# Block-sparse attention and a gated MLP in one program: w_in's raw words in their parts' place, fetched five tiles ahead; w_out's store on SyncE; a pair's last values and turns behind the next pair's scores

## The chip, the cores and the metric

The kernel runs on one core of one Trainium2 chip. The metric is the device time of one execution in microseconds (us). One execution was also recorded by the hardware profiler, with every instruction of the five engines (TensorE = PE, VectorE = DVE, ScalarE = ACT, GpSimd = POOL, SyncE = SP) and every DMA.

## The reference, cut to what matters

```python
# q, k, v: (4, 8, 768, 64); block = 32, 24 blocks of queries and keys; 3 sampled blocks a row of blocks
scores = scale * q @ k.T
mask   = |blk_i - blk_j| <= 1, or blk_i / blk_j is the first or last block, or blk_j is sampled for blk_i
attn   = softmax(where(mask, scores, -1e9))
x      = (attn @ v) as (3072 tokens, 512)
h      = x @ w_in                                   # (512, 2048)
g      = h * (1.0 / (1.0 + np.exp(-1.702 * h)))
return g @ w_out                                    # (2048, 512)
```

The weights come as 64-bit floats; the kernel gets their raw words and makes 32-bit parts of them.

## The kernel before, in words

**Tokens and chunks.** The 3072 tokens are 48 units of 64 tokens (two blocks of queries each); 8 units make a chunk of 512 tokens, and there are 6 chunks. 44 units are sparse: one item of work each, which reads 8 gathered key blocks (tile `kg`) and the matching value rows (`vown`, gathered by index, and `vmid`, the fixed ones). The other units, first and last block, are dense and have several items.

**An item** has four PE parts. `scores` (L262, 32 matmuls into two PSUM banks) is followed by `least` on DVE (L285, four instructions: bias and row minimum) and `exps` on ACT (L297, four). `transposes` (L313, eight) turns the exponentials over, and ACT copies them out of two PSUM banks (L318, two copies into `wst` or `pt` tiles). `values` (L339, 64 matmuls) is followed by `normalise` on DVE (L381). `turn` (L392, two transposes) is followed by ACT's copy `xhi` (L399) and DVE's remainder `xlo` (L400), which the MLP reads.

**Order.** The order of the instructions on each engine is written out by hand: it is the order in which the Python code issues them. Each engine works its own queue strictly in that order, and DMAs wait on the queue of the engine that issues them.

**The stage of pairs**, `first()`: chunk 0's eight items go in four pairs. A pair's two `scores` come first, then DVE and ACT work on both, then both items' `transposes`, both items' `values`, both `turn`s. Each pair shares one entry of keys and one of values. Both rings have two places (`RING = 2`): `loads()` issues the loads of a new entry once the code has issued the last reader of the one whose place it takes (the DMA then waits for that reader). Loads of `vown` stand on POOL's queue, those of `vmid`, `qt` and most of `kg` on SP's. `hold()` keeps some loads back until a pair's row minima exist.

**The ticks**, `tick(m)`: after the pairs, tick m does one slice of 128 of the 2048 hidden columns for one chunk: `up` (L495 to L497, 12 matmuls), `gate` (ACT L503, L508; DVE L510), and `down` of the slice before. There are 16 ticks a chunk. While chunk c is in the MLP, chunk c+1's items are put between the ticks' matmuls by `plan()`, always at the same ticks: scores in one tick, transposes in the next, values of an item behind the scores of the following one. In chunk 0, `down` is a 32-bit matmul (L540); from chunk 1 on it uses split parts (L552, L556, L557).

**The weights**, the generator `weights()` (`self.conv`): while chunk 0 is in the MLP, 32 tiles of raw words, alternately w_in and w_out (`todo`), are made into 32-bit parts. For tile k: `fetch(k)` issues a DMA of 512 KB on POOL's queue into one of three `raw` buffers (L422); `first(k)` is an ACT instruction that reads the words (L434); DVE shifts (L444), merges the high word (L451) and the low word (L458). For w_in ACT copies the high part into `win[f]` (L461) and DVE writes the remainder (L448). For w_out the whole word is kept, and a DMA on POOL's queue stores it to `ws[f]` (L464), from where later chunks read it. `next(self.conv)` issues one step of this; `weights(n)` in `first()` and `run(n)` in `tick()` say how many. Before tile k's steps the code calls `fetch(k + 2)`; the buffer that it takes is the one that tile k - 1 has just been read from. `first(k + 1)` is issued in the middle of tile k's steps, so ACT's queue stands still there if tile k + 1's words have not landed.

Of the kernel before, what the change touches and what calls it, by code (L numbers as in the profile page):

```python
# [18 lines left out]
P = 128  # L19
# [19 lines left out]
BIG = float(2 ** 33)  # L39
SCALE = 1.0 / float(D) ** 0.5  # L40
REBASE = 2.0 ** -112


class Kernel:
# [4 lines left out]
    def __init__(self, ctx, tc, q, qd, kb, kT, v, vd, sb, w_in, w_out, out):  # L49
# [15 lines left out]
        self.qt = [c.tile([P, 2, NPAIR * UT], F32, name=f"qt{i}") for i in range(RING)]  # L65
        self.vown = [c.tile([P, 2, 2 * DM], F32, name=f"vown{i}") for i in range(RING)]
        self.vmid = [c.tile([P, 2 * DM], F32, name=f"vmid{i}") for i in range(RING)]
        self.win = [c.tile([P, 2 * DM], F32R, name=f"win{f}") for f in range(NF)]
        self.wout = [c.tile([P, 2 * DM], F32R, name=f"wout{i}") for i in range(WRING)]
        self.x = [(c.tile([P, NCT, CT], F32R, name=f"xhi{i}"), c.tile([P, NCT, CT], F32R, name=f"xlo{i}"))  # L70
                  for i in range(2)]
# [334 lines left out]
    def weights(self):  # L406

        nc = self.nc
        todo = []
        for f in range(NF + LAG):  # L410
            if f < NF:
                todo.append((f, 0))
            if f >= LAG:
                todo.append((f - LAG, 1))
        self.ready = set()
        tiles = {}

        def fetch(k):
            if k < len(todo):
                f, i = todo[k]  # L420
                raw = self.work.tile([P, 2 * DM], I32, name="raw", bufs=3)
                nc.gpsimd.dma_start(out=raw, in_=self.w64[i][f])  # L422
                tiles[k] = {"raw": raw.rearrange("p (a b) -> p a b", b=2)}

        def first(k):


            f, i = todo[k]
            if i == 0:
                a = self.work.tile([P, DM], I32, name="a")  # L430
            else:
                a = self.work.tile([P, DM], F32R, name=("ghi", "glo")[f % 2]).bitcast(I32)
            tiles[k]["a"] = a
            nc.scalar.activation(out=a.bitcast(F32), in_=tiles[k]["raw"][:, :, 1].bitcast(F32), func=AF.Abs, scale=REBASE)  # L434

        fetch(0)
        fetch(1)
        yield
        first(0)
        for k, (f, i) in enumerate(todo):  # L440
            fetch(k + 2)
            raw, a = tiles[k]["raw"], tiles[k]["a"]
            low, high = raw[:, :, 0], raw[:, :, 1]
            nc.vector.tensor_scalar(out=a, in0=a, scalar1=3, scalar2=None, op0=ALU.logical_shift_left)  # L444
            yield
            if k > 0 and todo[k - 1][1] == 0:
                t, w = self.win[todo[k - 1][0]], tiles[k - 1]["a"].bitcast(F32)
                nc.vector.tensor_tensor(out=t[:, DM:2 * DM], in0=w, in1=t[:, 0:DM].bitcast(F32), op=ALU.subtract)  # L448
                self.ready.add(todo[k - 1])
                yield  # L450
            nc.vector.scalar_tensor_tensor(out=a, in0=high, scalar=-0x80000000, in1=a, op0=ALU.bitwise_and,  # L451
                                           op1=ALU.bitwise_or)
            if k + 1 < len(todo):
                while todo[k + 1][1] == 1 and (not self.turned or todo[k + 1][0] - 4 > self.downs - 1):
                    yield
                first(k + 1)
            yield
            nc.vector.scalar_tensor_tensor(out=a, in0=low, scalar=29, in1=a, op0=ALU.logical_shift_right,  # L458
                                           op1=ALU.bitwise_or)
            if i == 0:  # L460
                nc.scalar.copy(out=self.win[f][:, 0:DM], in_=a.bitcast(F32))  # L461
            else:
                self.whole[f] = a.bitcast(F32)
                nc.gpsimd.dma_start(out=self.ws[f], in_=self.whole[f])  # L464
                self.ready.add((f, i))
            yield

# [210 lines left out]
    def first(self):  # L678
# [5 lines left out]
        def finish(todo):  # L684
            for f in todo:
                f()
# [5 lines left out]
        def hold(g, k):  # L692

            nc.gpsimd.tensor_copy(out=self.seen[:, 0:NPAIR], in_=g["unit"]["nm"][:, 0])
            self.vmost = k

        for p in range(CU // 2):
            pair = items[2 * p:2 * p + 2]
            exps = [self.scores(g) for g in pair]
            exps[0][0]()  # L700
            finish(exps[0][1:])
            exps[1][0]()
            exps[1][1]()
            if p == 0:
                hold(pair[1], CU // 2)
            if p == CU // 2 - 1:
                hold(pair[0], CU // 2 + 1)
                nc.sync.dma_start(out=self.seen[:, NPAIR:2 * NPAIR], in_=pair[0]["unit"]["nm"][:, 0])
                self.kmost = CU // 2 + 1
            self.loads()  # L710
            behind = [self.transposes(pair[0])]
            behind[0][0]()
            exps[1][2]()
            finish(behind[0][1:])
            behind.append(self.transposes(pair[1]))
            if p == CU // 2 - 1:
                self.turned = True
                weights(2)
            finish(behind[1])
            after = [self.values(g) for g in pair]  # L720
            finish(after[0])
            finish(after[1])
            self.loads()
            for g in pair:
                finish(self.turn(g))
            if p > 0:
                weights((1, 3, 2)[p - 1])

    def run(self):
        self.g, self.wst, self.whole, self.downs = {}, {}, {}, 0  # L730
# [63 lines left out]
```

## Time and profile before

| | |
|---|---|
| time, median of 3 runs | 803.52 us (802.85 to 808.4) |
| time of the profiled execution | 802.63 us |
| its span, first to last instruction | 801.0 us |
| PE, DVE, ACT, POOL busy | 755.8, 396.7, 365.4, 77.3 us |
| mean granted clock of TensorE | 0.980 |
| DMA | 128.20 MB, 160 GB/s over the span |

Busy shares are averages over stages that have different limits, so the rows further down are taken by stage: the pairs end where the first `up` starts, at 65.86 us; chunk 0's ticks end where the first split `down` (L556) starts, at 229.26 us; the rest is chunks 1 to 5. A wait is shown by who waited, for whom, and how long; a chain of waits is followed back from an end to what released each step.

### The profile page before, as it was taken

The numbers are of one execution on the slowest core, as the hardware profiler recorded it, in microseconds if no ns is written. First come the engines' busy times: TensorE is split into PE (matmuls) and PEld (weight loads), VectorE is DVE, ScalarE is ACT, GpSimd is POOL, SyncE is SP. The second block draws the span as 40 slices with busy tenths as digits, with TensorE's granted clock in tenths as the row PEclk, the third lists the DMA queues.
The fourth block names the chain that finished last, engine by engine and source line by source line (L and its number), as shares of the span: only waits on it lengthen the run. The fifth ranks groups of instructions, "written<-read, shape, count | busy, mean of one in ns | idle before, by whom it ended". The sixth has DMA issues, their size and how long they took to land.

```text
span 801.0 us, 19132 instructions
## 1 busy us (share of the span) xinstructions
PE 755.8 (94%) x7520; PEld 563.5 (70%) x7520; DVE 396.7 (50%) x1044; ACT 365.4 (46%) x919; POOL 77.3 (10%) x125
## 2 busy tenths in 40 slices
PE   3778799799999999999999999999999999999997
PEld 2545555565677777777878778778777777788885
DVE  4366667666355453454454454444555444443333
ACT  2464555444454545354444454454455444332332
POOL 3422222230000000000000000000000000000000
PEclk9889899899999999999999999999999999999999
DMA  8959877685574254655444365354574222132111
GB/s 259 296 184 348 256 256 226 238 283 162 156 246 158 76 161 150 204 155 171 137 122 159 117 170 175 112 179 119 159 244 157 89 70 75 41 92 54 40 53 52
DMA packets 61211, 128.20 MB, mean 160 GB/s; under 512 B 7713, under 2 KB 27938, under 8 KB 60610
## 3 DMA queue, kind: packets, MB, share of 16 engines
q1 hardware_dynamic: 47650, 80.90, 33.6%
q0 software_dynamic: 12656, 45.23, 17.0%
q8 instruction: 59, 0.97, 0.5%
q10 hardware_dynamic: 816, 0.86, 0.4%
q14 instruction: 30, 0.25, 0.1%
HBM read 116.47 MB, written 10.49 MB: 158 GB/s over the span
## 4 chain that ended last, share of the span: by engine, by line
PE 81%; DMA 8%; DVE 4%; ACT 3%; issue 3%; SPq 1%; POOL 0%; ACTq 0%; POOLq 0%; DVEq 0%
PE bank L495 11%; PE bank L497 10%; PE bank L496 10%; PE bank L556 9%; PE bank L557 9%; PE bank L552 9%; PE bank L339 5%; PE bank L313 5%; PE bank L262 5%; DMA raw<-in_moe_w_out_dram 3%; PE bank L540 3%; PE bank L347 2%; PE bank L274 2%; DMA raw<-in_moe_w_in_dram 1%; DMA kg<-in_kb_dram 1%
## 5 line engine op out<-in xcount | busy, mean ns | idle before, releaser
L495 PE MATMUL bank<-xhi,win 128*128 128x512 f32 x384 | 162.0, 422 | 1.9 <-ACT wst L508 1.3
L497 PE MATMUL bank<-xhi,win 128*128 128x512 f32 x384 | 151.1, 393 | 0.1
L496 PE MATMUL bank<-xlo,win 128*128 128x512 f32 x384 | 151.0, 393 | 0.0
L510 DVE SCALAR_TENSOR_TENSOR g<-g,bank 128x512 f32<-128x512 f32 x83 | 57.1, 687 | 187.6 <-ACT g L503 187.6
L297 ACT ACTIVATE ex<-bank,nm 128x256 f32<-128x256 f32 (+1 forms) x176 | 84.6, 489 | 123.7 <-DVE nm L285 122.0
L556 PE MATMUL bank<-wout,ghi 128*128 128x512 f32 x320 | 128.4, 401 | 0.0
L503 ACT ACTIVATE g<-bank 128x512 f32<-128x512 f32 x96 | 57.4, 598 | 153.7 <-PE bank L497 153.7
L557 PE MATMUL bank<-wout,ghi 128*128 128x512 f32 x320 | 126.7, 396 | 0.0
L484 DVE TENSOR_TENSOR wout<-wst,wout 128x512 fp32r<-128x512 f32 x80 | 55.4, 692 | 78.2 <-ACT wout L483 77.3
L552 PE MATMUL bank<-wout,glo 128*128 128x512 f32 x320 | 89.8, 394 | 0.0
L495 PEld LDWEIGHTS bank<-xhi,win 128*128 128x128 f32 x384 | 72.4, 188 | 23.9 <-ACT wst L508 3.2
L497 PEld LDWEIGHTS bank<-xhi,win 128*128 128x128 f32 x384 | 72.3, 188 | 16.1
L285 DVE CUSTOM_DVE_ANT_1 bank<-bank,bias 128x256 f32<-128x256 f32 x176 | 73.7, 441 | 19.9 <-PE bank L262 16.9
L496 PEld LDWEIGHTS bank<-xlo,win 128*128 128x128 f32 x384 | 72.5, 189 | 15.0 <-issue 2.2
L218 POOL DMA_INDIRECT vown<-in_v_dram,vidx x44 | 43.4, 986 | 390.1 <-PE bank L339 272.4
L262 PE MATMUL bank<-kg,qt 64*32 64x256 f32 x1408 | 55.2, 404 | 23.8 <-DMA kg<-in_kb_dram 12.5
L517 ACT CAST ghi<-g 128x512 fp32r<-128x512 f32 x80 | 49.6, 621 | 45.4 <-DVE g L510 45.4
L552 PEld LDWEIGHTS bank<-wout,glo 128*128 128x128 f32 x320 | 60.1, 188 | 14.5
L318 ACT COPY pt<-bank 128x512 f32<-128x512 f32 (+1 forms) x112 | 57.2, 562 | 28.1 <-PE bank L313 28.1
L557 PEld LDWEIGHTS bank<-wout,ghi 128*128 128x128 f32 x320 | 60.2, 188 | 13.7
L556 PEld LDWEIGHTS bank<-wout,ghi 128*128 128x128 f32 x320 | 60.1, 188 | 13.5
L262 PEld LDWEIGHTS bank<-kg,qt 64*32 64x32 f32 x1408 | 26.4, 111 | 47.6 <-issue 20.2
(103 smaller groups left out, 942.6 us busy)
## 6 DMA issues: line engine op xcount, KB each, us to landing
wst<-ws SPq DMA_DIRECT2D x80, 256.0 KB, 2.7
kg<-in_kb_dram SPq DMA_DIRECT2D x142, 128.0 KB, 3.5
kg<-in_kb_dram SPq DMA_DIRECT2D x22, 384.0 KB, 4.9
raw<-in_moe_w_in_dram POOLq DMA_DIRECT2D x16, 512.0 KB, 5.7
raw<-in_moe_w_out_dram POOLq DMA_DIRECT2D x16, 512.0 KB, 5.9
kg<-in_kT_dram SPq DMA_DIRECT2D x4, 1536.0 KB, 8.3
vown<-in_vd_dram SPq DMA_DIRECT2D x8, 768.0 KB, 4.5
qt<-in_q_dram SPq DMA_DIRECT2D x22, 256.0 KB, 3.4
```

Of the source, the lines that this page charges most:

```text
L262: nc.tensor.matmul(sps[h][BLK * c:BLK * (c + 1), n * i:n * (i + 1)].rearrange("p (n s) -> p n s", s=BLK), self.qt[r][rows, bi, UT * pair + ...
L285: nc.vector.tensor_tensor_reduce(out=at, in0=at, in1=bias, scale=-SCALE, scalar=3.0e38, op0=ALU.add, op1=ALU.min, accum_out=un["nm"][:, ha ...
L297: nc.scalar.activation(out=ex, in_=sps[h][:, n * k:n * (k + 1)], func=AF.Exp, bias=un["nm"][:, half, c:c + 1], scale=-1.0, accum_out=un["r ...
L318: copies.append(lambda pt=pt, ps=ps, m=m: nc.scalar.copy(out=pt[:, 0:m], in_=ps[:, 0:m]))
L495: nc.tensor.matmul(h, wih[:, k], hi[:, k], start=(k == 0), stop=False)
L496: nc.tensor.matmul(h, wih[:, k], lo[:, k], start=False, stop=False)
L497: nc.tensor.matmul(h, wil[:, k], hi[:, k], start=False, stop=(k == NCT - 1))
L503: nc.scalar.activation(out=g, in_=self.h, func=AF.Tanh, scale=0.851)
L510: nc.vector.scalar_tensor_tensor(out=g, in0=g, scalar=1.0, in1=h, op0=ALU.add, op1=ALU.mult)
L552: nc.tensor.matmul(o[n], glo[:, tk[n]], woh, start=False, stop=last)
L556: nc.tensor.matmul(o[n], ghi[:, tk[n]], woh, start=(f == 0), stop=False)
L557: nc.tensor.matmul(o[n], ghi[:, tk[n]], wol, start=False, stop=False)
```

## The change

`AHEAD = 5`: five fetches are issued at once, and tile k's steps begin with `fetch(k + 5)`. The raw words of w_in no longer go through the `raw` buffers: they land in the place of `win[f]` itself (the same const tile, as integers), and the tile of parts is allocated over it after the low words have been read. The three `raw` buffers are left to w_out's words. A further `yield` stands behind `first(0)`. The store of w_out's tile to `ws[f]` is issued by SyncE instead of GpSimd.

In `first()`, a pair ends with its first item's `values`. The second item's `values` and both `turn`s come behind the next pair's `scores`. Both items' `exps` are now all issued ahead of the first copy out of the transposes. `loads()` is called once for each pair instead of twice. Steps of `weights` are issued at other places: the fetches at the end of the third pair (before: of the second), the rest in and behind the last pair; no step of `weights` is left between the third pair and the fourth pair's scores.

```diff
+AHEAD = 5
...
-        self.win = [c.tile([P, 2 * DM], F32R, name=f"win{f}") for f in range(NF)]
+        self.win = [None] * NF
...
         def fetch(k):
             if k < len(todo):
                 f, i = todo[k]
-                raw = self.work.tile([P, 2 * DM], I32, name="raw", bufs=3)
+                if i == 0:
+                    raw = self.const.tile([P, 2 * DM], I32, name=f"win{f}")
+                else:
+                    raw = self.work.tile([P, 2 * DM], I32, name="raw", bufs=3)
                 nc.gpsimd.dma_start(out=raw, in_=self.w64[i][f])
...
-        fetch(0)
-        fetch(1)
+        for k in range(AHEAD):
+            fetch(k)
         yield
         first(0)
+        yield
         for k, (f, i) in enumerate(todo):
-            fetch(k + 2)
+            fetch(k + AHEAD)
...
             if i == 0:
+                self.win[f] = self.const.tile([P, 2 * DM], F32R, name=f"win{f}")
                 nc.scalar.copy(out=self.win[f][:, 0:DM], in_=a.bitcast(F32))
             else:
                 self.whole[f] = a.bitcast(F32)
-                nc.gpsimd.dma_start(out=self.ws[f], in_=self.whole[f])
+                nc.sync.dma_start(out=self.ws[f], in_=self.whole[f])
...
+        prev = None
         for p in range(CU // 2):
-            pair = items[2 * p:2 * p + 2]
-            exps = [self.scores(g) for g in pair]
+            a, b = items[2 * p:2 * p + 2]
+            final = p == CU // 2 - 1
+            exps = [self.scores(g) for g in (a, b)]
+            after, turned = (self.values(prev[1]), self.turn(prev[0])) if p else ([], [])
             exps[0][0]()
             finish(exps[0][1:])
             exps[1][0]()
-            exps[1][1]()
+            finish(exps[1][1:])
+            finish(after)
...
             self.loads()
-            behind = [self.transposes(pair[0])]
-            behind[0][0]()
-            exps[1][2]()
-            finish(behind[0][1:])
-            behind.append(self.transposes(pair[1]))
-            if p == CU // 2 - 1:
+            behind = self.transposes(a)
+            finish(turned)
+            if p:
+                finish(self.turn(prev[1]))
+            if final:
+                weights(1)
+            finish(behind)
+            behind = self.transposes(b)
+            if final:
                 self.turned = True
                 weights(2)
-            finish(behind[1])
-            after = [self.values(g) for g in pair]
-            finish(after[0])
-            finish(after[1])
-            self.loads()
-            for g in pair:
-                finish(self.turn(g))
-            if p > 0:
-                weights((1, 3, 2)[p - 1])
+            finish(behind)
+            if final:
+                weights(1)
+            finish(self.values(a))
+            if p == CU // 2 - 2:
+                weights(1)
+            prev = a, b
+        after = self.values(b)
+        turned = self.turn(a)
+        finish(after)
+        finish(turned)
+        finish(self.turn(b))
+        weights(3)
```

## Rows read from the trace of the kernel before

**Rows 1.** Busy time by stage (the windows view): stretch in us, its length, busy us and (x) instructions of PE, PE's weight loads, DVE, ACT, POOL, then granted TensorE clock, DMA share, GB/s.

```profile
12.48:65.86 53.38, 40.16 (x848) 27.87 (x848) 25.86 (x101) 28.09 (x92) 13.84 (x20) 0.84 0.84 264
65.86:229.26 163.40, 149.79 (x1445) 93.77 (x1446) 104.92 (x258) 79.60 (x200) 36.69 (x56) 0.96 0.73 237
229.26:801.00 571.74, 565.89 (x5229) 441.81 (x5227) 261.55 (x659) 256.20 (x628) 20.60 (x22) 1.00 0.42 127
```

**Rows 2.** The page's fourth part, the chain that ended last over the whole span, by line.

```profile
PE bank L495 11%; PE bank L497 10%; PE bank L496 10%; PE bank L556 9%; PE bank L557 9%; PE bank L552 9%; PE bank L339 5%; PE bank L313 5%; PE bank L262 5%; DMA raw<-in_moe_w_out_dram 3%; PE bank L540 3%; PE bank L347 2%; PE bank L274 2%; DMA raw<-in_moe_w_in_dram 1%; DMA kg<-in_kb_dram 1%
```

**Rows 3.** Waits of ACT between 64 and 205 us: who waited for whom, us in total, times, longest.

```profile
ACT a L434 <- DMA raw<-in_moe_w_in_dram: 15.1, 8, 4.7
...
ACT ghi L434 <- DMA raw<-in_moe_w_out_dram: 10.4, 4, 4.7
...
ACT glo L434 <- DMA raw<-in_moe_w_out_dram: 5.9, 2, 4.2
```

**Rows 4.** Four links of the chain of waits, in order of time: start us, us, what.

```profile
81.09 5.69 DMA raw<-in_moe_w_in_dram
86.86 0.66 ACT a L434
87.52 0.48 ACT pt L318
88.04 2.44 PE bank L262 x32
```

**Rows 5.** The largest wait of PE between 64 and 205 us.

```profile
PE bank L262 <- ACT pt L318: 10.1, 4, 4.3
```

**Rows 6.** The windows view of two stretches right behind such waits (columns as in rows 1; the last three are clock, DMA share, GB/s).

```profile
88.04:93.40 5.36, 5.36 (x98) 3.19 (x99) 4.82 (x14) 4.20 (x12) 0.67 (x2) 0.50 0.80 254
152.65:158.30 5.65, 5.65 (x99) 3.75 (x100) 5.51 (x18) 2.92 (x10) 1.07 (x2) 0.50 0.62 200
```

**Rows 7.** Two items' scores on PE's timeline: start us, us, line, out<-in, count, idle time before and its releaser.

```profile
105.15 1.09 PE L262 MATMUL bank<-kg,qt 64*32 64x256 f32 x32
...
134.64 1.78 PE L262 MATMUL bank<-kg,qt 64*32 64x256 f32 x32 [1.40 <-ACT pt L318]
```

**Rows 8.** Waits of POOL between 64 and 205 us.

```profile
POOL ws L464 <- DVE ghi L458: 34.7, 7, 10.5
POOL ws L464 <- DVE glo L458: 23.4, 7, 5.5
POOL raw L422 <- issue: 13.9, 4, 7.8
```

**Rows 9.** DMA issues: engine, count, KB each, median us from issue to landing.

```profile
raw<-in_moe_w_in_dram POOLq DMA_DIRECT2D x16, 512.0 KB, 5.7
```

**Rows 10.** PE's timeline in the stage of pairs: the second pair's values, the scores of the third and of the fourth pair, the fourth pair's first transposes, the first `up`.

```profile
34.64 0.28 PE L339 MATMUL bank<-vmid,wst 128*32 128x64 f32 x1 [0.39 <-DMA vmid<-in_v_dram]
...
39.78 1.58 PE L262 MATMUL bank<-kg,qt 64*32 64x256 f32 x46
...
51.70 2.07 PE L262 MATMUL bank<-kg,qt 64*32 64x256 f32 x64
...
65.86 0.50 PE L495 MATMUL bank<-xhi,win 128*128 128x512 f32 x1 [0.46 <-ACT xhi L399]
```

**Rows 11.** DVE's timeline: the first `least` of the third pair; the first word step behind the third pair, and the first `least` of the fourth.

```profile
41.00 0.43 DVE L285 CUSTOM_DVE_ANT_1 bank<-bank,bias 128x256 f32<-128x256 f32 x1 [0.28 <-PE bank L262]
...
52.81 0.43 DVE L444 TENSOR_SCALAR a<-a 128x512 int32<-128x512 int32 x1 [0.17 <-ACT a L434]
...
54.61 0.42 DVE L285 CUSTOM_DVE_ANT_1 bank<-bank,bias 128x256 f32<-128x256 f32 x1
```

**Rows 12.** Groups by line in the stage of pairs, 12 to 66 us: shapes, count, busy us, mean ns of one, idle before.

```profile
L297 ACT ACTIVATE glo<-bank,nm 128x256 f32<-128x256 f32 x16 | 7.5, 483 | 0.0
...
L318 ACT COPY pt<-bank 128x512 f32<-128x512 f32 x8 | 4.9, 608 | 2.6 <-PE bank L313 2.6
...
L399 ACT CAST xhi<-bank 128x256 fp32r<-128x256 f32 x8 | 3.0, 372 | 12.8 <-PE bank L392 12.8
...
L434 ACT ACTIVATE a<-raw 128x512 f32<-128x512 f32 x2 | 1.3, 698 | 0.0
...
L448 DVE TENSOR_TENSOR win<-a,win 128x512 fp32r<-128x512 f32 x1 | 0.7, 684 | 0.0
```

**Rows 13.** SP's queue: the load of the second pair's `vmid`; the first loads of the fifth and of the seventh entry of keys.

```profile
25.58 1.14 SPq L216 DMA_DIRECT2D vmid<-in_v_dram  x2
...
57.15 0.54 SPq L189 DMA_DIRECT2D qt<-in_q_dram  x1
...
90.59 0.34 SPq L189 DMA_DIRECT2D qt<-in_q_dram  x1
```

**Rows 14.** PE's weight loads of the ninth item's scores, which wait for the fifth entry of keys.

```profile
70.34 0.60 PEld L262 LDWEIGHTS bank<-kg,qt 64*32 64x32 f32 x28 [0.92 <-DMA kg<-in_kb_dram]
```

**Rows 15.** The windows view once more, for the DMA (last two columns: share, GB/s).

```profile
0.00:50.00 50.00, 29.36 (x613) 20.26 (x617) 20.61 (x97) 20.44 (x66) 17.19 (x43) 0.90 0.92 286
50.00:57.00 7.00, 3.90 (x104) 2.76 (x94) 5.33 (x18) 3.82 (x10) 0.18 (x1) 0.92 0.02 8
57.00:85.00 28.00, 22.67 (x231) 14.37 (x229) 17.72 (x44) 13.91 (x38) 8.50 (x12) 0.90 0.95 315
85.00:200.00 115.00, 104.76 (x1067) 64.76 (x1068) 79.06 (x193) 57.27 (x139) 27.00 (x44) 0.94 0.71 235
```

More of the change, by code (lines that the diff above doesn't have):

```diff
@@ L702, in first @@
             exps[1][0]()
-            exps[1][1]()
+            finish(exps[1][1:])
+            finish(after)
             if p == 0:
-                hold(pair[1], CU // 2)
-            if p == CU // 2 - 1:
-                hold(pair[0], CU // 2 + 1)
-                nc.sync.dma_start(out=self.seen[:, NPAIR:2 * NPAIR], in_=pair[0]["unit"]["nm"][:, 0])
+                hold(b, CU // 2)
+            if final:
+                hold(a, CU // 2 + 1)
+                nc.sync.dma_start(out=self.seen[:, NPAIR:2 * NPAIR], in_=a["unit"]["nm"][:, 0])
                 self.kmost = CU // 2 + 1
             self.loads()
-            behind = [self.transposes(pair[0])]
-            behind[0][0]()
-            exps[1][2]()
-            finish(behind[0][1:])
-            behind.append(self.transposes(pair[1]))
-            if p == CU // 2 - 1:
+            behind = self.transposes(a)
[7 more added lines that the diff above has]
+            if final:
                 self.turned = True
                 weights(2)
-            finish(behind[1])
-            after = [self.values(g) for g in pair]
-            finish(after[0])
-            finish(after[1])
-            self.loads()
-            for g in pair:
-                finish(self.turn(g))
-            if p > 0:
-                weights((1, 3, 2)[p - 1])
+            finish(behind)
+            if final:
+                weights(1)
[9 more added lines that the diff above has]
+        weights(3)
     def run(self):
```

## The prediction

> **What bounds the kernel now.** I read the windows by stage first. From 229.26 us on, PE is busy 565.89 of 571.74 us at clock 1.00 [rows 1]; the change touches nothing there, so those 572 us stay. In chunk 0's ticks PE is busy 149.79 of 163.40 us at a mean clock of 0.96: 13.6 us stand idle, and part of the rest runs slow. In the stage of pairs it is busy 40.16 of 53.38 us. So at most some 25 to 30 us are to be had, all of them ahead of 229 us.
>
> Then the chain of waits: over the whole span it is PE but for two DMAs, w_out's words 3% and w_in's 1% [rows 2], about 32 us of 801. ACT's waits show the same: 15.1 + 10.4 + 5.9 = 31.4 us for raw words [rows 3]. How an ACT wait reaches PE is seen at 81 us [rows 4]: the words are issued at 81.09 and land 5.69 us later, ACT reads them at 86.86, and only then comes the copy out of the transposes, which stood behind that instruction in ACT's queue; PE's next scores wait for the copy and start at 88.04. PE's largest wait in the stage is this one, 10.1 us in 4 times [rows 5].
>
> After the two longest of these waits PE runs at clock 0.50, the lower of its two levels, for 5.36 and 5.65 us, busy throughout [rows 6]. Scores that take 1.09 us at full clock [rows 7] take 2.44 there [rows 4]. At full clock the two stretches would take half: (5.36 + 5.65) / 2 = 5.5 us are lost.
>
> Why the words come late: POOL's queue. A fetch goes out at most two tiles ahead and takes the buffer of the tile just read; POOL stands 13.9 us in all before such fetches, and 34.7 + 23.4 us before the stores of w_out, with the next fetch queued behind [rows 8]. Landing takes 5.7 us in the median [rows 9]. 32 tiles in 163.40 us is some 5 us a tile, so a lead of under two tiles, less those waits, is about what a landing takes.
>
> **Part 1: five ahead, w_in in its own place.** w_in's fetch now waits for no buffer. w_out's takes one of three; its last user is tile k - 1, whose low-word step has just been issued. The lead becomes nearly 5 x 5 = 25 us against a landing of 6. It adds no instruction and no byte. I take all 31.4 us of ACT's waits as gone, and with them PE's 13.6 us of idle time and the 5.5 us of low clock, for there would be no waits left to set them off. What could then be late next is DVE, 104.92 us busy, or ACT, 79.60 us [rows 1], against a PE floor of 163.40 - 13.6 - 5.5 = 144.3 us; a tick has the same steps as before. Both stay under PE. Bounds: nothing gained if the words still come late (a rival below), 19.1 if all goes.
>
> **Part 2: the store on SyncE.** 16 DMA issues move from POOL to SP. On POOL the wait for DVE's low word no longer stands ahead of fetches and of `vown`'s gathers. On SP it now stands ahead of `qt`, `kg` and `vmid` loads of chunk 1. What that costs: the seventh entry of keys starts loading at 90.59 [rows 13]; the fifth took from 57.15 to 70.34 until its readers went [rows 13, 14], 13.2 us; so the seventh has landed by some 104 us, and its first reader is the scores at 134.64 [rows 7]. The slack is 30 us, the longest wait of a store 10.5 us [rows 8]. I cost it at nothing; if that slack were gone, up to 10.5 us for a store.
>
> **Part 3: the pairs.** Going by the new order, a pair from its scores: `least` starts 1.22 us behind them (39.78 to 41.00) at 0.43 a piece [rows 10, 11]; two of these on, at 2.3, ACT starts its eight exponentials (0.48 each) and ends at about 6.1; two `xhi` copies follow (0.37 each), partly pipelined, then the first item's two copies (0.6 each) until 7.9 [rows 12]. The second item's transposes must wait for these banks, then come the first item's `values`; by the 1.0 us of an item's scores [rows 7] I estimate 1.8 for both. That is 9.7 us to the next pair's scores, where before it was 51.70 - 39.78 = 11.92. The gain can't be had three times, for the value rows are late: the second pair's `values` wait for `vmid` until 34.64 [rows 10], issued at 25.58 [rows 13] on a queue whose order up to there does not change. DMA is busy 0.92 of the first 50 us [rows 15]. So I keep 34.64: first item's `values` to 35.7 = scores of the third pair (before 39.78); scores of the fourth 35.7 + 9.7 = 45.4 (before 51.70).
>
> The last pair took 65.86 - 51.70 = 14.16 us [rows 10]. Of these `least` started late: 54.61 - 51.70 = 2.91 instead of 1.22, since DVE's word steps from 52.81 stood ahead [rows 11]; 1.7 us go. Two ACT reads of words (0.70 each) and one copy (0.6) now come in that stretch, 2.0 more [rows 12]; the first item's `values` go ahead of the second's copies, 1.0 less. 14.16 - 1.7 + 2.0 - 1.0 = 13.5, so the first `up` is at 58.9 instead of 65.86: 7.0 us. Bounds: if `vmid` comes 4 us sooner, 11; if the third pair's scores do not move, 3.
>
> **What is given back.** The remainder of `win[0]` is no longer ready ahead of the first `up`: a shift and L448, 0.4 + 0.7, less what the first two matmuls cover: 0.6 us. The fifth entry of keys is needed at about 58.9 + 3.5 = 62.4; its loads wait for the fourth pair's first minima, so for about 45.4 + 3, and 13.2 us more give 61.6, now with five tiles of words beside it on the DMA: 1.5 us, between 0 and 6. The first `up` keeps 0.5 us of wait for `xhi` [rows 10]. Together 2.6.
>
> **Sum.** The profiled execution's own time is 802.63 us for a span of 801.0; the 1.6 us around it stay. 802.6 - 7.0 - 13.6 - 5.5 + 2.6 = 779.1. The runs' median, 803.52, is 0.9 above that execution: 780.0.
>
> **A rule that speaks against it.** The DMA's rate in the busy stretch from 57 to 85 us is 315 GB/s at share 0.95 [rows 15]; fetching earlier moves bytes, it does not make them fewer. The Trainium skill ("DMA: Bandwidth & Descriptors", "Where 436 GB/s comes from") puts the limit that HBM sets at some 358 GB/s a core, and ("Queues, rings and completion order") says that each DMA engine goes round the queues that have work, packet by packet. So words fetched early would take turns with the keys that PE needs next. That 65.86 to 85 us is full agrees; that 50 to 57 us is nearly empty (0.02) does not. By that figure the second rival below would end at about 782.
>
> **The rivals.**
> - *The pairs gain nothing* (the loads of the last value rows, now issued behind the previous pair's late `values`, set the end): `up` stays at 65.86, the ticks gain their 19.1 less 2.1. 802.6 - 17.0 + 0.9 = 786.5. For it: DMA share 0.92 until 50 us. Against: the last entry's loads start behind the second pair's second `values`, at about 35.7 + 2.1 + 1 = 38.8, and are needed only by the fourth pair's `values`, behind 54.
> - *The DMA is the bound up to 85 us.* From 50 to 85 us the kernel before moved 7 us at 8 GB/s and 28 us at 315, together 8.9 MB [rows 15]; three tiles more ahead are 1.6 MB. 10.5 MB at 315 GB/s take 33.3 us, so the point that the kernel before reached at 85 us is reached at 83.3: 1.7 us gained by then. Behind it 115 - 104.76 = 10.2 us of idle and 5.5 of clock [rows 15, 6], and the DMA has room (0.71). 802.6 - 17.4 + 0.9 = 786. Against: the extra tiles are not needed at that moment, the keys are, and the empty hole from 50 to 57 us fills.
> - *The lead does not come about*: POOL's gathers wait for PE, the fetches behind them lose their lead, ACT still waits. Then only the pairs gain: 802.6 - 7.0 + 0.9 = 796.5. Against: such a wait must eat 25 us.
> - *Slower*: SP's stores hold up the loads of chunk 1. The stores waited 34.7 + 23.4 us on POOL; if all of it reached PE, 802.6 - 23.5 + 58 + 0.9 = 838. It decides from some 32 us on (the gain and 1% more), that is if more than half of the stores' waits cost PE as much; the slack of 30 us an entry speaks against.
>
> **Chances.** The forecast 0.62, no gain in the pairs 0.12, DMA-bound start 0.12, no lead 0.09, slower 0.05. Likeliest own range 774 to 784. For 8 in 10 I go from 771 (pairs gain 11, nothing given back but 0.6) to 790 (both middle rivals in part). About 1%, 8 us, is what a measurement of this kernel can tell from no change: faster 0.87, same 0.08, slower 0.05.
>
> **What the profile would show.** First `up` at 57 to 61 us, the fourth pair's scores near 45, no L434 wait for raw words over 1 us, PE idle below 4 us between the first `up` and the first L556, clock 1.00 there, some 145 us between the two; POOL's waits for L458 gone to SP, and no `kg` load late for PE but the fifth entry's. Wrong if `kg` or `vmid` take the place of raw in PE's waits, or if the fourth pair's scores wait for DMA.

## The result, and the profile after

The changed kernel takes 784.55 us (median of 4 runs, 783.86 to 784.94) where the kernel before took 805.03 beside it (802.85 to 808.4): a ratio of 0.9741, interval 0.9702 to 0.9781. The forecast was 780.0, range 771 to 790. The profiled execution took 784.16 us, its span 782.5; before it was 802.63 and 801.0.

The windows by stage of the changed kernel, in the columns of [rows 1]: pairs, chunk 0's ticks, the rest.

```profile
11.36:60.98 49.62, 36.57 (x849) 26.64 (x849) 24.09 (x99) 27.58 (x92) 15.94 (x25) 0.90 0.96 311
60.98:207.42 146.44, 143.66 (x1445) 91.13 (x1445) 105.30 (x260) 79.16 (x199) 25.68 (x36) 0.99 0.78 257
207.42:782.50 575.08, 569.25 (x5231) 442.11 (x5229) 261.75 (x659) 256.61 (x628) 20.66 (x22) 1.00 0.42 126
```

Against [rows 1]: the pairs are 3.8 us shorter (53.38 to 49.62) and start 1.1 us sooner, the ticks are 16.7 shorter, and the rest, in which no instruction was changed, is 3.1 us *longer*. (For the last two, before is counted to the record of the first L556, at 229.02 instead of 229.26, as here to the first L562: 163.16 and 571.98 us.) The sum is -18.5 us, the difference of the two profiled times. How long the pairs take differs from one execution to the next: in the four profiles with the old order, of this kernel and of those below, they take 52.7 to 55.1 us, and 46.6 to 50.2 in the eight with the new order in which no load of keys or values is moved.

The page's chain by line, to set beside [rows 2]: no DMA of raw words is left in it. (L501 to L503 are `up`, L546 is the 32-bit `down`, L558 to L563 the split one.)

```profile
PE bank L501 13%; PE bank L503 11%; PE bank L502 11%; PE bank L562 10%; PE bank L558 10%; PE bank L563 10%; PE bank L546 7%; PE bank L314 6%; PE bank L340 5%; PE bank L263 5%; DMA kg<-in_kb_dram 2%; PE bank L348 2%; PE bank L275 2%; DMA vmid<-in_v_dram 1%; PE bank L393 1%; DMA vown<-in_v_dram,vidx 1%
```

All waits of PE in the ticks, 60.98 to 207.42 us. The wait for ACT's copies, 10.1 us in [rows 5], is gone; ACT has no wait for raw words at all, where it had 31.4 us [rows 3]. What is left is one wait for loads, in tick 1.

```profile
PE bank L263 <- DMA vmid<-in_v_dram: 2.0, 1, 2.0
PE bank L501 <- ACT xhi L400: 0.5, 1, 0.5
PE bank L503 <- DVE win L453: 0.4, 1, 0.4
PE bank L263 <- DMA kg<-in_kb_dram: 0.3, 1, 0.3
```

PE's timeline, to set beside [rows 10] and [rows 14]: the second pair's values, the third pair's scores, a stop in the middle of the second pair's last values, the fourth pair's scores, the first `up`, and the ninth item's scores in tick 1 in two parts.

```profile
34.70 0.29 PE L340 MATMUL bank<-vmid,wst 128*32 128x64 f32 x1 [1.21 <-DMA vmid<-in_v_dram]
...
36.56 2.50 PE L263 MATMUL bank<-kg,qt 64*32 64x256 f32 x64
...
41.87 0.22 PE L340 MATMUL bank<-vmid,pt 128*32 128x64 f32 x1 [1.92 <-issue]
...
46.81 0.96 PE L263 MATMUL bank<-kg,qt 64*32 64x256 f32 x22
...
60.98 0.49 PE L501 MATMUL bank<-xhi,win 128*128 128x512 f32 x1 [0.46 <-ACT xhi L400]
...
66.99 0.62 PE L263 MATMUL bank<-kg,qt 64*32 64x256 f32 x4 [2.02 <-DMA vmid<-in_v_dram]
...
67.94 1.53 PE L263 MATMUL bank<-kg,qt 64*32 64x256 f32 x28 [0.33 <-DMA kg<-in_kb_dram]
```

The wait for `vmid` in the second pair ends at 34.70, as it did before at 34.64. The first `up` comes at 60.98 instead of 65.86, but the ninth item's scores go on at 67.94 instead of 70.34: half of those 4.9 us is handed back in tick 1, and the stretch behind that wait runs at a mean clock of 0.57, near the lower of the two levels:

```profile
67.94:71.50 3.56, 3.56 (x33) 2.23 (x34) 1.98 (x5) 0.62 (x1) 2.03 (x3) 0.57 0.87 279
```

### The profile page after: what moved, and what is told of

Same layout as the page of the kernel before. It is cut to its first block, busy times and chain, and to the rows that moved or that the text cites. A ratio compares the mean times of both kernels' runs of the same rounds, so it can differ in the third digit from the quotient of the medians.

```text
span 782.5 us, 19089 instructions
## 1 busy us (share of the span) xinstructions
PE 749.5 (96%) x7520; PEld 559.9 (72%) x7520; DVE 395.5 (51%) x1044; ACT 364.8 (47%) x919; POOL 68.4 (9%) x109
## 4 chain that ended last, share of the span: by engine, by line
PE 92%; DMA 5%; SPq 1%; issue 1%; DVE 0%; POOL 0%; ACT 0%; POOLq 0%; DVEq 0%
PE bank L501 13%; PE bank L503 11%; PE bank L502 11%; PE bank L562 10%; PE bank L558 10%; PE bank L563 10%; PE bank L546 7%; PE bank L314 6%; PE bank L340 5%; PE bank L263 5%; DMA kg<-in_kb_dram 2%; PE bank L348 2%; PE bank L275 2%; DMA vmid<-in_v_dram 1%; PE bank L393 1%; DMA vown<-in_v_dram,vidx 1%
## 5 line engine op out<-in xcount | busy, mean ns | idle before, releaser
L501 PE MATMUL bank<-xhi,win 128*128 128x512 f32 x384 | 164.4, 428 | 0.6 <-ACT xhi L400 0.5
L503 PE MATMUL bank<-xhi,win 128*128 128x512 f32 x384 | 152.1, 396 | 0.4 <-DVE win L453 0.4
L562 PE MATMUL bank<-wout,ghi 128*128 128x512 f32 x320 | 128.6, 402 | 0.0
L563 PE MATMUL bank<-wout,ghi 128*128 128x512 f32 x320 | 126.3, 395 | 0.0
L558 PE MATMUL bank<-wout,glo 128*128 128x512 f32 x320 | 90.1, 395 | 0.0
L501 PEld LDWEIGHTS bank<-xhi,win 128*128 128x128 f32 x384 | 72.5, 189 | 21.6 <-issue 2.7
L503 PEld LDWEIGHTS bank<-xhi,win 128*128 128x128 f32 x384 | 72.4, 189 | 18.7 <-DVE win L453 0.7
L502 PEld LDWEIGHTS bank<-xlo,win 128*128 128x128 f32 x384 | 72.6, 189 | 16.5 <-issue 2.6
L558 PEld LDWEIGHTS bank<-wout,glo 128*128 128x128 f32 x320 | 60.1, 188 | 14.7
L562 PEld LDWEIGHTS bank<-wout,ghi 128*128 128x128 f32 x320 | 60.2, 188 | 13.8
L563 PEld LDWEIGHTS bank<-wout,ghi 128*128 128x128 f32 x320 | 60.2, 188 | 13.5
L263 PE MATMUL bank<-kg,qt 64*32 64x256 f32 x1408 | 52.0, 399 | 15.3 <-DMA kg<-in_kb_dram 13.2
L531 DVE TENSOR_TENSOR glo<-g,ghi 128x512 fp32r<-128x512 f32 x80 | 54.7, 684 | 0.7 <-ACT ghi L523 0.7
```

The lines of the kernel that those rows point to most:

```text
L263: nc.tensor.matmul(sps[h][BLK * c:BLK * (c + 1), n * i:n * (i + 1)].rearrange("p (n s) -> p n s", s=BLK), self.qt[r][rows, bi, UT * pair + ...
L501: nc.tensor.matmul(h, wih[:, k], hi[:, k], start=(k == 0), stop=False)
L502: nc.tensor.matmul(h, wih[:, k], lo[:, k], start=False, stop=False)
L503: nc.tensor.matmul(h, wil[:, k], hi[:, k], start=False, stop=(k == NCT - 1))
L558: nc.tensor.matmul(o[n], glo[:, tk[n]], woh, start=False, stop=last)
L562: nc.tensor.matmul(o[n], ghi[:, tk[n]], woh, start=(f == 0), stop=False)
```

## The experiments

Four questions: what the ticks' gain comes from (lead, buffers, store or pairs), why the pairs gained 3.8 us and not 7, where the 3.1 us behind the ticks went, and whether the wait in tick 1 can be had back. Each run was timed beside the kernel before; a row of the windows view under a run is that of its ticks or of what lies behind them, in the columns of [rows 1].

### The parts of the change

**The kernel before once more** (no edit).

> The kernel before, unchanged, for its stages on this chip. In the two profiles so far the stretch behind chunk 0's ticks, which the change does not touch, took 571.7 us before and 575.1 after. If that is the chip, the two are told apart by nothing in the program and this run may show either; if it comes from the change (another place of the weight parts in memory), this run shows 571 to 572 again and every kernel with the parts' new place 575. Ratio 1.00 in both.

Measured: ratio 0.9999 (0.9969 to 1.003). Behind the ticks 572.03 us, as in the first profile of before (571.98). The ticks took 167.49 us where the first profile had 163.16: the waits for raw words differ from one execution to the next (38.4 us of ACT's time here, 31.4 there), and so does the kernel's time, 802.07 to 809.88 us.

```profile
65.68:233.17 167.49, 150.83 (x1444) 93.87 (x1445) 104.71 (x258) 79.64 (x199) 37.08 (x56) 0.95 0.71 230
233.17:805.20 572.03, 566.17 (x5231) 442.01 (x5229) 261.89 (x659) 256.61 (x628) 20.68 (x22) 1.00 0.42 127
```

**The fetches alone**, on the kernel before:

```diff
-        self.win = [c.tile([P, 2 * DM], F32R, name=f"win{f}") for f in range(NF)]
+        self.win = [None] * NF
...
+                if i == 0:
+                    raw = self.const.tile([P, 2 * DM], I32, name=f"win{f}")
+                else:
+                    raw = self.work.tile([P, 2 * DM], I32, name="raw", bufs=3)
...
-        fetch(0)
-        fetch(1)
+        for k in range(5):
+            fetch(k)
...
-            fetch(k + 2)
+            fetch(k + 5)
...
+                self.win[f] = self.const.tile([P, 2 * DM], F32R, name=f"win{f}")
```

> Kernel before plus the five fetches ahead and w_in's own place; the store stays on GpSimd, the pairs stay in their old order. Theory (the lead of the fetches pays in the ticks, by itself): no wait for raw words, first up at 64 to 66 us, ticks 146 to 149 us instead of 163.4, ratio 0.978 to 0.984. Rival (the store of w_out on GpSimd's queue was what held the fetches): the stores still stand ahead of fetches, half of the ticks' gain at most, ratio 0.989 or more.

Measured: 789.32 us, ratio 0.9787 (0.9757 to 0.9818). No wait for raw words; the ticks take 144.84 us, with the store still on GpSimd's queue: 1.2 us less than the theory's lower bound. The first `up` comes at 67.29, 1.3 us later than its upper one. The ratio is in the range, and the rival falls.

```profile
67.29:212.13 144.84, 142.38 (x1445) 90.37 (x1445) 104.28 (x258) 79.17 (x199) 34.02 (x52) 1.00 0.77 254
212.13:787.30 575.17, 569.25 (x5231) 442.09 (x5229) 261.84 (x659) 256.71 (x628) 20.65 (x22) 1.00 0.42 126
```

**The pairs alone**: the changed kernel's `first()` with the old buffers, two fetches ahead, the store on GpSimd.

```diff
-AHEAD = 5
+AHEAD = 2
...
-        self.win = [None] * NF
+        self.win = [c.tile([P, 2 * DM], F32R, name=f"win{f}") for f in range(NF)]
...
-                nc.sync.dma_start(out=self.ws[f], in_=self.whole[f])
+                nc.gpsimd.dma_start(out=self.ws[f], in_=self.whole[f])
```

> The new order of the pairs alone: two fetches ahead through the old buffers, the store on GpSimd. Theory: first up at 60 to 62 us, but the ticks keep their waits for raw words and take 160 us or more; ratio 0.992 to 0.998. Rival (a stage of pairs that ends earlier leaves room on the DMA and pays in the ticks too): ticks below 155 us, ratio below 0.985.

Measured: 794.94 us, ratio 0.9874 (0.9825 to 0.9922). The pairs take 49.61 us, as in the changed kernel, first `up` at 61.91; the ticks take 156.66 us, between the two expectations. ACT still waits 32.5 us for raw words, but PE's longest single wait for a copy is 2.3 us where it was 4.3, and the clock 0.98 instead of 0.96. So the new order is worth more than the pairs' own time: against the three profiles of the kernel before and of its padded form (163.16, 167.49 and 164.05 us) the ticks are 6.5 to 10.8 us shorter. Why is not shown: this run also has the fetches and the steps of `weights` at their new places in the pairs. The gains do not add: against 805.78 us, the median of before beside both, the fetches alone give 16.5 us and the pairs alone 10.8; the whole change gave 20.5. That fits both taking time from the same waits. Behind the ticks it is 572.03 us, with the parts in their old place.

```profile
61.91:218.57 156.66, 148.14 (x1444) 93.00 (x1445) 105.51 (x260) 80.17 (x199) 36.77 (x56) 0.98 0.75 245
```

**Two ahead**, all else as changed (`AHEAD = 2`).

> The changed kernel with two fetches ahead instead of five; w_in's own place, the store on SyncE and the pairs' new order stay. Theory (the lead pays): ACT waits again for raw words, some 15 us or more, ticks 154 us or more, ratio 0.985 to 0.995. Rival (the buffers and the store were what held the fetches, two ahead would do): ticks at 146 to 149 us, ratio 0.974 as the changed kernel.

Measured: 790.74 us, ratio 0.9799 (0.9761 to 0.9836). ACT waits 6.4 us for w_in's words and 5.6 for w_out's, 12.0 in all, and the ticks take 153.19 us: waits, ticks and ratio all come out somewhat better than the theory said, and the ticks well above the rival's 149 us. In these profiles, with two ahead, place and store bring 156.7 to 153.2, 3.5 us; the lead from two to five brings 153.2 to 146.4, 6.8 us, of which 1.4 us is a longer wait for keys in tick 1 (3.7 us for 2.3). The first figure is loose: the pairs alone took 792.24 to 799.22 us, and the execution profiled was the fastest of them.

```profile
60.62:213.81 153.19, 146.86 (x1444) 92.78 (x1445) 105.36 (x260) 79.07 (x199) 24.17 (x36) 0.97 0.74 253
```

**The store back on GpSimd** (`nc.gpsimd.dma_start(out=self.ws[f], ...)`), all else as changed.

> The changed kernel with the store of w_out back on GpSimd's queue. Theory (the lead of 25 us covers a store's wait, so the store's queue pays nothing): first up at 60 to 62 us, ticks 145 to 148 us as in the changed kernel (146.4), no wait for raw words, ratio 0.973 to 0.977. Rival (the store's wait on GpSimd holds the fetches back): waits for raw words return, ticks 152 us or more, ratio 0.982 or more.

Measured: 785.41 us, ratio 0.9732 (0.9701 to 0.9763); ticks 147.25, no wait for raw words. Moving the store pays nothing that this can show.

```profile
60.92:208.17 147.25, 143.59 (x1444) 90.89 (x1445) 105.14 (x260) 79.22 (x199) 34.61 (x52) 0.99 0.78 255
```

### What the parts' place costs behind the ticks

In three profiles so far (before, before once more, the pairs alone) the stretch behind the ticks takes 572.0 us, in five (the changed kernel, the fetches alone, two ahead, the store back, and the keys early below) 575.1 to 575.3, and which it is goes with one thing alone: whether `win` is allocated ahead of the small constant tiles or behind them. By the compiled program's list of tiles, `win0` starts at byte 69760 of its partition before, a multiple of 64, and at 116512 in the changed kernel, 32 beyond one; `ghi` and `glo` start 32 beyond a multiple of 64 in both.

**The parts in front again**, the words still landing in them (the other constant tiles, `wout` and the x tiles among them, go back to their old places too, 65,536 bytes on, which changes no start's remainder by 64 or 128):

```diff
         self.win = [None] * NF
+        self.place = [c.tile([P, 2 * DM], I32, name=f"win{f}") for f in range(NF)]
...
-                    raw = self.const.tile([P, 2 * DM], I32, name=f"win{f}")
+                    raw = self.place[f]
```

> The changed kernel, but the 16 places of w_in's parts are allocated where the kernel before had them, ahead of everything else that is constant: each starts at a multiple of 64 bytes in its partition, as before, and not at 32 beyond one. Nothing else differs. Theory (the 3.1 us that the untouched stretch behind the ticks lost come from the start of the weight tiles that the up matmuls load): that stretch takes 572.0 us again instead of 575.1, and the ticks 0.6 us less; ratio 0.970 to 0.972. Rival (the words landing in the parts' place, or the order of the program, is behind it): 575 us.

Measured: 779.02 us, ratio 0.9656 (0.963 to 0.9683), and 572.09 us behind the ticks. The ratio is below what was expected: the ticks are 1.4 us shorter instead of 0.6. In this profile the ninth item's scores wait for no load (66.26 us, in one piece), although nothing was done about that wait.

```profile
205.81:777.90 572.09, 566.13 (x5231) 441.98 (x5229) 261.89 (x659) 256.43 (x628) 20.59 (x22) 1.00 0.42 127
```

**32 bytes more** behind the last small tile:

```diff
         self.bias = const.tile([P, NU, 8], F32, name="bias")
+        const.tile([P, 8], F32, name="pad")
```

> The changed kernel with 32 bytes more behind the last small constant tile, so that the 16 places of w_in's parts and also all working tiles (ghi and glo, which the down matmuls load as weights, among them) start at multiples of 64 bytes. Theory: the up matmuls are as fast as in the kernel before (3.1 us less behind the ticks), and the down matmuls, whose weights started 32 bytes off in the kernel before too, gain about the same 3.3 ns a matmul, 960 of them, 3.2 us: the stretch behind the ticks takes 568 to 570 us, ratio 0.966 to 0.969. Rival (only where the tiles lie relative to each other matters, not their start): 572 or 575 us.

Measured: 776.91 us, ratio 0.9633 (0.9613 to 0.9654), and 568.18 us behind the ticks, the fastest of all kernels here; it beats the kernel before and the changed one, and by more than expected in all (0.966 to 0.969).

```profile
206.62:774.80 568.18, 562.36 (x5231) 442.08 (x5229) 260.91 (x659) 256.43 (x628) 20.59 (x22) 1.00 0.42 128
```

**The same pad in the kernel before**, nothing else.

> The kernel before with nothing but 32 bytes more behind the last small constant tile: the working tiles (ghi, glo and the others) start at multiples of 64 bytes; w_in's parts did already. Theory (the start of a weight tile costs each matmul that loads it some 3 ns): the stretch behind the ticks takes 568 to 569 us instead of 572.0, as in the changed kernel with the pad; pairs and ticks as before; ratio 0.993 to 0.997. Rival (the pad pays only together with the change): ratio 1.00, 572 us.

Measured: 799.89 us, ratio 0.9955 (0.9925 to 0.9985); behind the ticks 567.45 us.

```profile
230.15:797.60 567.45, 561.51 (x5231) 442.17 (x5229) 260.84 (x659) 256.58 (x628) 20.67 (x22) 1.00 0.42 128
```

575.1 - 572.0 = 3.1 us over the 78 x 12 = 936 `up` matmuls there is 3.3 ns each; 572.1 - 568.2 = 3.9 us is 4.1 ns each for the 80 x 12 = 960 `down` matmuls, if all of it is theirs. The traces say whose it is. Adding up the times from one matmul's start to the next one's behind the ticks, the `up` matmuls take 222.1 us in the kernel before and with the parts in front, 225.0 in the changed kernel, and 221.8 with the pad; the `down` matmuls take 228.9 in the first two, 229.2 in the changed kernel, and 225.4 with the pad; all other work of PE takes 115.3 in each. So 2.9 of the 3.1 us lie in the matmuls that load `win` as weights, and 3.5 of the 3.9 in those that load `ghi` and `glo`. That it is the start, and not which tiles lie next to each other, is shown by the pad in the changed kernel: it leaves the order as changed and takes the price away.

### The wait in tick 1 and the pairs

**Keys early**: the fifth entry of keys is loaded a pair sooner.

```diff
-                nc.sync.dma_start(out=self.seen[:, NPAIR:2 * NPAIR], in_=a["unit"]["nm"][:, 0])
-                self.kmost = CU // 2 + 1
+            if p == CU // 2 - 2:
+                self.kmost = CU // 2 + 1
             self.loads()
```

> The changed kernel with the fifth entry of keys loaded one pair earlier: its loads are issued behind the third pair's scores and no longer wait for the fourth pair's minima. Theory (the DMA stands nearly idle from 40 to 45 us because the fourth pair's value rows and the fetches wait for a place, and the keys for the tenth block of work come too late at 67 us): the hole fills, the scores in tick 1 wait for nothing, the low clock behind that wait goes too, ticks 141.5 to 143.5 us instead of 146.4, first up within 1 us of 61, 3 to 5 us faster than the changed kernel, ratio 0.968 to 0.971. Rival (the DMA is full there anyway, so the keys push the value rows or the words back): first up 2 us or more later, ticks unchanged, ratio 0.973 or more.

Measured: 786.57 us, ratio 0.9741 (0.9708 to 0.9774). The wait in tick 1 is gone, but the first `up` comes at 64.3 us, 3.3 later, and the DMA share in the pairs is 1.03 instead of 0.96: the rival holds. (Ticks 145.54 us, 0.9 less than in the changed kernel.)

**Three ahead, with the pad** (`AHEAD = 3`).

> The changed kernel with the pad and three fetches ahead instead of five (with the pad and five: 776.9 us, ticks 146.0). Theory (a lead of about 15 us still covers a landing of 6 to 10 us): no wait for raw words over 1 us, ticks 144.5 to 147 us, within 1.5 us of five ahead. Rival (five are needed, a landing behind keys and values takes longer): ticks 149 us or more, 780 us or more.

Measured: 779.06 us, ratio 0.9709 (0.9663 to 0.9756). One wait for raw words, 1.2 us: three ahead do cover the landing. But the ticks take 149.26 us, outside what the theory gave and where the rival had them (its 780 us or more did not come), since the ninth item's scores wait 5.3 us for keys; the first `up` had come sooner, at 59.04, and they go on at 69.12. It was the keys, not the words.

```profile
PE bank L264 <- DMA kg<-in_kb_dram: 5.3, 2, 5.1
```

**Two fetches first, three later, with the pad**:

```diff
-        for k in range(AHEAD):
+        for k in range(2):
             fetch(k)
         yield
         first(0)
         yield
+        for k in range(2, AHEAD):
+            fetch(k)
```

> The changed kernel with the pad; of the first five fetches only two are issued at the end of the third pair, the other three behind the fourth pair's key and value loads on GpSimd's queue. Theory (the words fetched early delay the fifth entry of keys, whose readers wait 2 to 3 us in tick 1 and start a stretch of low clock): that wait goes, ticks 143 to 145 us instead of 146.0, 1 to 3 us faster than with the pad alone. Rival (keys and words share the DMA whatever the order): ticks 145.5 us or more, no difference over 1 us.

Measured: 780.43 us, ratio 0.971 (0.9656 to 0.9764); the wait in tick 1 is not gone, those scores go on at 70.24, and the ticks take 148.81 us, 2.8 more than with the pad alone. What was to come of the edit did not come, and the rival's "no difference" did not either. But the run does not test the theory: the three fetches do not go out behind the fifth entry's keys, but beside them. SyncE issues those loads from 50.65 to 59.8 us, and GpSimd six fetches from 53.2 to 56.5, where with the pad alone it issues three there and five from 44.4 to 47.1; the DMA's share from 50 to 55 us is 0.62 instead of 1.04.

**The second entry of values from the start, with the pad** (`self.vmost = 2` at the beginning).

> The changed kernel with the pad; the second entry of values is loaded from the start, ahead of the third entry of keys, instead of behind the first pair's minima. Theory (the pairs gain only 4 us, not 7, because the second pair's values wait for vmid until 34.7 us): its values start at 31 to 33 us, the first up at 57 to 59.5 us instead of 60.6, 1 to 3 us faster than with the pad alone. Rival (the DMA is full, so what comes sooner for one comes later for the next): the second pair's scores wait for keys 1 us or more longer, first up at 60 us or later, no gain.

Measured: 782.16 us, ratio 0.9738 (0.9688 to 0.9789). The second pair's scores now wait until 28.28 us, the first `up` comes at 69.7, and the ticks take 143.57 us, without a wait in tick 1. The rival holds, and more so than it said. PE's timeline: the second pair's scores, and the stop in the second pair's last values.

```profile
28.28 3.89 PE L264 MATMUL bank<-kg,qt 64*32 64x256 f32 x64 [6.39 <-DMA vmid<-in_v_dram]
...
46.86 0.26 PE L341 MATMUL bank<-vmid,pt 128*32 128x64 f32 x1 [5.28 <-issue]
```

The loads up to tick 1 look like one account: in the changed kernel and the kernels with the pad alone and with three ahead, the ninth item's scores go on at 67.9, 67.8 and 69.1 us whether the first `up` was at 61.0, 60.6 or 59.0. None of the three ways to move one load against another (keys, fetches, values) won time by it. But the wait also differs between kernels whose loads were not touched there: those scores go on at 66.3 us with the parts in front, without a wait, and at 68.8 with the store back on GpSimd. With one profile of each, a difference of some 2 us in tick 1 can't be put down to an edit.

## Why the prediction was right, and by how much it missed

The profiled execution took 784.16 us for a forecast of 779.1. The 5 us come from two places: the first `up` is 2.1 us later than forecast, and the stretch behind the ticks 3.3 us longer; the ticks are 0.5 us shorter.

**The ticks: right.** The waits for raw words went, all of them; the ticks were to fall to 163.4 - 19.1 + 2.6 = 146.9 us and took 146.44. That the two agree so well is in part luck, since two errors cancel. The low clock cost more than the 5.5 us that were priced from the two longest stretches: PE's busy time fell by 5.9 us (149.55 to 143.66) although tick 1 put some 1.5 us back, and in the fetches alone, at a clock of 1.00, it is 142.38. And more was given back than 2.6 us (below). That the lead does it stands on two runs: the fetches alone reach 144.84 us with the store still on GpSimd, and the changed kernel with two ahead has 12.0 us of such waits again. DVE and ACT stayed under PE as forecast (105.30 and 79.16 us of 146.44). A landing of w_in's words became longer, 8.3 us in the median for 5.7, and the lead covered it.

**The store: right at nothing**, in both directions: 147.25 against 146.44 us of ticks. SyncE's queue took the waits over (between 20 and 210 us, SP's largest wait before a store, in six times, is below), and no load but the one in tick 1, which stands ahead of all stores on that queue, was late for PE.

```profile
SPq L470 <- DVE a L449: 29.6, 6, 6.5
```

**The pairs: the mechanism right, the term mis-sized**: the first `up` was to come 7.0 us sooner and comes 4.9 sooner, 1.1 of it because the pairs start sooner and 3.8 because they are shorter. The third pair's scores came at 36.56 (forecast 35.7, from a wait for `vmid` that ended at 34.70 as kept); the fourth's at 46.81, 10.25 later instead of 9.7, with a stop of 1.92 us in the values (last section), where the kernel before has one of 0.53 us in the scores; the first `up` 14.17 us behind them instead of 13.5. "14.16 - 1.7 + 2.0 - 1.0" took too much off: the last pair is as long as it was.

**What is given back: 1.5 us was too little.** Tick 1's scores wait 2.3 us for loads, and the low clock behind that (0.57 for 3.56 us) was not in the sum; since the full level would save 0.43 x 3.56, it is another 1.5 us. By the prediction's own sign this is a small part of being wrong: loads of `kg` and `vmid` are now the largest wait of PE in the ticks, 2.3 us where the idle time was 13.6. The second rival, the DMA as the bound, was put on everything up to 85 us and did not come about as that: from 75 us on PE waits for nothing. It reckoned with 315 GB/s, and the limit that the prediction cites lies lower than what was moved too: the changed kernel moved 400, 403 and 386 GB/s in the three stretches of 5 us from 50 us on, at a share of 1.03 to 1.05. In the small, loads are what PE waits for up to 68 us; that the full DMA is why two of the three attempts (keys and values) won nothing fits their later first `up`, and is argued.

```profile
50.00:55.00 5.00, 2.43 (x15) 1.47 (x15) 3.69 (x15) 5.00 (x20) 3.83 (x6) 0.98 1.03 400
55.00:60.00 5.00, 4.56 (x137) 3.90 (x135) 1.99 (x6) 2.66 (x6) 0.00 (x0) 0.68 1.03 403
60.00:65.00 5.00, 4.00 (x14) 2.38 (x14) 4.03 (x10) 1.56 (x3) 0.00 (x0) 1.00 1.05 386
```

**The step that failed**: "the change touches nothing there, so those 572 us stay". It touches where `win` lies. Two lines of the diff move the allocation of the 16 tiles behind the small constant ones, and PE takes 3.1 us longer over the same 5,231 instructions. With the parts in front it is 779.02 us, within 1 us of the forecast of 780.0; that is in part luck too, since the first `up` (60.79 us) is still 1.9 us late there and the ticks (145.02 us) as much shorter than forecast. The prediction named the lines and priced them at no instruction and no byte, which is so; none of the rows it was made from shows the price.

**The rivals.** By its time alone, 784.55 us lies nearer to the 786 and 786.5 us of the first two rivals than to the forecast; it is the stages that decide. No gain in the pairs: 2.1 of the 7.0 us failed to come. No lead: excluded by the fetches alone. Slower by SyncE's queue: excluded by the store's run.

## What to carry to other kernels

Price a fetch's lead against its landing *and* against what the issuing queue stands before; here a lead of two tiles was worth some 7 us less than five, and a third one covered the words. When an edit changes which tile is allocated when, compare the tiles' start addresses in the compiled program, and the length of a stretch that the edit does not touch: a difference there is a hint that costs nothing to read. Where loads fill the DMA, moving one ahead can move another back, as with the keys and the values here; look for the sum's end, not for the wait that went.

## What was not expected of the hardware

**A weight tile's start.** Weights of 128x128 that start 32 bytes beyond a multiple of 64 cost a 128x512 matmul some 3 to 4 ns, 0.4 to 0.5% of this kernel for each of the two kinds. The changed kernel's rows (stretch 240 to 740 us) and those of the kernel with the pad show it in the mean of the two lines of `down` (first two rows; third and fourth with the pad), though these means say less than the length of the stretch:

```profile
L562 PE MATMUL bank<-wout,ghi 128*128 128x512 f32 x276 | 111.0, 402 | 0.0
L563 PE MATMUL bank<-wout,ghi 128*128 128x512 f32 x276 | 108.9, 395 | 0.0
```

```profile
L563 PE MATMUL bank<-wout,ghi 128*128 128x512 f32 x278 | 110.6, 398 | 0.0
...
L564 PE MATMUL bank<-wout,ghi 128*128 128x512 f32 x278 | 108.8, 392 | 0.0
```

The Trainium skill ("SBUF — State Buffer", "Operand start alignment") asks only that an operand start at a multiple of its element size, and says that this is about legality and not speed. All starts here are such multiples, and the runs show a price all the same. Whether 64 is the step that counts, and not a coarser one, stays open: 69760 is a multiple of 64 and of 128, 116544 (the pad) of 64 alone. With the pad in both, `win` at the first place gives 220.9 us from start to start for the 936 `up` matmuls and 567.45 us behind the ticks (one profile), at the second 221.8 and 568.2 to 568.3 (four): 1 ns a matmul, which a start at a multiple of 64 alone may still cost.

**A stop of PE without a wait.** In the second pair's last values PE stands for 1.92 us, with the pad alone for 0.42 and in the kernel of the last experiment for 5.28, in each behind 24 of the 32 matmuls of `vmid` with `pt`; no engine and no load of data ends it. It does not belong to these matmuls. In all fourteen traces PE stands, for 0.1 to 5.3 us, behind its 470th matmul, whatever comes next: in the kernel before it is one of the third pair's scores.

```profile
41.89 1.02 PE L262 MATMUL bank<-kg,qt 64*32 64x256 f32 x18 [0.53 <-issue]
```

The DMA records of the queue that the page calls `instruction` go with it:

```profile
q8 instruction: 59, 0.97, 0.5%
```

In each trace PE goes on 1.4 to 1.9 us after the third of these packets, of 16,384 bytes, has landed: at 41.87 after 40.28 us in the changed kernel, at 46.86 after 45.44 in the last experiment. So the likely cause is that PE waits for a piece of its own program. No run moved that packet by itself, so this is argued, and why it comes late in the last experiment stays open.
